# The first phase of a fused sparse-attention and ELU feed-forward kernel: eleven blocks' min-and-subtract step and one batch's v copies on GpSimd, with its DMA issues dealt out between them

## The chip, the cores and the metric

One core of a Trainium2 chip runs the whole program. The metric is device time in microseconds (us) of one execution; the time of a kernel is the median of its runs.

Five engines work side by side and meet only through semaphores: TensorE (PE, with its weight loads PEld), VectorE (DVE), ScalarE (ACT), GpSimd (POOL) and SyncE (SP). Each takes its own instructions strictly in order, so an instruction that waits holds up all that stand behind it on its engine. POOL and SP also issue DMAs; the transfers themselves run on 16 DMA engines.

## The reference

Attention over 8 batches, 8 heads, 576 positions, 64 features, followed by a feed-forward layer on its output. Heads 0 to 3 are local (a key is seen if it lies 0 to 31 positions back), heads 4 to 7 are strided (a key is seen if it lies a multiple of 32 positions back, or is the position itself).

```
scores = q @ k.T / 8, masked by head
attn   = softmax(scores);  x = attn @ v          # x: 4608 tokens x 512
h = x @ w_in                                      # 512 -> 2048
g = where(h > 0, h, exp(min(h, 0)) - 1)           # ELU
out = g @ w_out                                   # 2048 -> 512
```

## The kernel before

**Tiles and phases.** The 4608 tokens are nine chunks of 512. For a chunk `nb` the feed-forward layer has 16 blocks `m` of 128 hidden features. `moe_in` makes one block's hidden values `hps` in a PSUM bank with four 128x512 matmuls (L622); `moe_act` makes the ELU of it into `g_sb`; `moe_out` multiplies four blocks of `g_sb` at a time by `w_out_sb` (L667, four matmuls), and after four of those the result is copied (L671) and stored. A loop over `nb` and, inside, over slots `s` = 0 to 15 writes the order of all engines out by hand: in slot `s` comes block `m = s`, and two half-slots (`2s`, `2s+1`) of the next batch's attention, taken from the table `gaps` that `attention(nb + 1, ...)` makes. So while chunk 0 is worked on (the first phase), batch 1's attention runs between its blocks; batch 0's attention runs before the loop, in the hand-written order `OPENING`.

**The ELU of a block.** ACT makes `e_sb = exp(hps)` (L648). DVE then makes `e1_sb = min(e_sb, 1) - 1` (L655, the min and subtract step) and `g_sb = max(e1_sb, hps)` (L657). For five blocks of chunk 0, those in `ON_SCALAR` (4, 7, 10, 13, 15), it goes another way: ACT makes `e1_sb = relu(hps)` (L651) and DVE makes `min(e_sb - 1, e1_sb)` in one instruction (L652). `e_sb` and `e1_sb` have three buffers each.

**What ties PE to the others.** The banks for `hps` are a ring: three in slots 0 to 9 of chunk 0 (two "half" tiles and one "single"), two from slot 10 on. Block m's matmuls wait until the block that had the bank before has been through L657 or L652. In chunk 0 only the first three groups of `moe_out` are taken in the phase itself, at the ends of slots 11, 13 and 15 (they need blocks 0 to 3, 4 to 7 and 8 to 11); the fourth, which needs blocks 12 to 15, comes right after block 0 of chunk 1.

**The attention pieces.** A pair is two heads; `s0`, `s1` (strided) and `l0`, `l1` (local) for one batch. Pieces of a pair: transposes of q and k on PE (L361, L375) with copies out of PSUM (L364, L378), scores (L493) and their exp (L501, on ACT), the mask product on DVE (L516), the product with v (`av`, L535), its reciprocal and scaling on DVE (L543, L544, into `x_s` or `x_l`), and the transposes of that back on PE (L571, L584) with copies into `xT`. For the strided heads v is first copied from the landing tile `v_raw` into `v_str` (`v_in`, L414): for batch 1 on ACT, for later batches on DVE. `halo` (L421) copies the ends of local v rows.

**POOL's queue.** All loads but the first are issued from POOL in program order: strided tensors in five DMAs each (four of 108 rows, L178, and one for the rest, L182), local ones in one each (L189, L195), the weights `w_in_sb` in four slices (L316) and `w_out_sb` in four (L728). Eight semaphores go round among POOL's DMAs, so that each issue waits for the landing of the DMA eight places earlier. After batch 1's loads stand, in this order: the slices 2 and 3 of `w_in`, the four of `w_out`, memsets of batch 2's tiles (`clear_v(2)`, `clear_nat(2)`, L246 to L248 and L238), batch 2's loads (`load_batch(2)`, 18 DMAs), six small memsets (`clear_loc`, L243), batch 3's loads.

Of the kernel before, what the change touches and what calls it, by code (L numbers as in the profile page):

```python
# [13 lines left out]
ALU = mybir.AluOpType  # L14
# [28 lines left out]


OPENING = """
s0.cast_q s0.t_q s0.t_k s1.cast_q s1.t_k s0.s0 s0.m0 s1.t_q s0.s1 s0.m1 fill.2 l0.t_q s1.s1
s1.m1 s1.s0 s1.m0 l0.t_k l1.t_q fill.1 s0.v l0.s0 l0.m0 l1.t_k l0.s1 s1.a0 s0.a0 l0.m1 l1.s0
s1.a1 s0.a1 fill.1 l1.s1 l1.m0 fill.1 s1.halo s1.x fill.1 s0.x l1.m1 fill.1 l0.a0 fill.1 l0.a1
l1.a0 moe.2 l1.a1 S0.t_q l0.x S1.t_q moe.3 l1.x moe.0 moe.1
""".split()  # L50
ON_VECTOR = "s0.t_q s1.cast_q s1.t_k l0.t_q s0.v l1.x".split()


ON_SCALAR = (4, 7, 10, 13, 15)
AHEAD = 3


# [1 line left out]
def kernel(  # L59
# [9 lines left out]
    nc = tc.nc  # L69
    B, H, S, D = q.shape  # L70
# [93 lines left out]
    raw = {}  # L164
    src = {"q": q, "k": k, "v": v}

    def load_strided(b, name, engine=nc.gpsimd, heads=range(4)):
# [9 lines left out]
        for h in heads:  # L177
            engine.dma_start(out=t[0:108, h].rearrange("p g d -> p (g d)"),  # L178
                             in_=rows[h, :, 0:30, :].rearrange(
                                 "t (r g) d -> t r (g d)", g=5))  # L180
            if h == 1:
                engine.dma_start(  # L182
                    out=t[108:126, :, 0:2, :].rearrange("p h g d -> p h (g d)"),
                    in_=rows[:, :, 30:32, :].rearrange("h t g d -> t h (g d)"))

    def load_local(b, name):
        if name == "v":
# [35 lines left out]
    def load_batch(b):  # L223
        for name in "qkv":
            load_strided(b, name)
        for name in "qkv":
            load_local(b, name)

    def rows_of(t, h):

        return t[0:126, h, 0:2, :], t[0:108, h, 2:5, :]


    def clear_nat(i, engine=nc.vector):

        for name in "kq":
# [24 lines left out]
    for i in range(2):  # L261
# [17 lines left out]
                            op=ALU.subtract)  # L279
# [44 lines left out]
    load_local(1, "q")  # L324
    load_local(1, "k")
    load_local(1, "v")
    load_w_in(2)


    class Pair:  # L330
        def __init__(self, b, strided, hp):
            self.b, self.strided, self.hp = b, strided, hp
            self.kind = "s" if strided else "l"
            self.h2 = slice(2 * hp, 2 * hp + 2)
            self.name = f"{self.kind}{hp}"
            self.pr, self.x = {}, None

        def copy(self, step, late):

# [68 lines left out]

        def v_in(self, part):

            if self.strided and self.hp == 0:
                o = rows_of(v_str[self.b % 3][:, :, :, 0:D], slice(0, 4))[part]
                i = rows_of(raw[self.b], slice(0, 4))[part]
                self.copy("v", self.b > 1)(o, i)  # L414

        def halo(self):

# [172 lines left out]
    def attention(b, start, pitch, at):  # L590


        gaps = {}
        pairs = [Pair(b, s, hp) for s in (b < EARLY, b >= EARLY) for hp in range(2)]
        begin = start if b >= EARLY else [start + pitch * i for i in range(4)]
        if b >= EARLY:
            gaps[begin[0]] = [pairs[3].halo]
        for i, pr in enumerate(pairs):
            if b == 1 and pr.strided:
                pr.t_q = lambda: None  # L600
# [12 lines left out]


    g_of = {}
# [29 lines left out]
    def moe_act(nb, m):  # L645
        hps = hps_of[m]
        e_sb = p_e.tile([128, N_TILE], F32, tag="e_sb", name="e_sb")
        nc.scalar.activation(e_sb, hps, ACT.Exp)  # L648
        e1_sb = p_e.tile([128, N_TILE], BF16, tag="e1_sb", name="e1_sb")
        if nb == 0 and m in ON_SCALAR:  # L650
            nc.scalar.activation(e1_sb, hps, ACT.Relu)  # L651
            nc.vector.scalar_tensor_tensor(g_of[nb][:, m, :], e_sb, 1.0, e1_sb,  # L652
                                           op0=ALU.subtract, op1=ALU.min)
            return
        nc.vector.tensor_scalar(e1_sb, e_sb, scalar1=1.0, scalar2=1.0,  # L655
                                op0=ALU.min, op1=ALU.subtract)
        nc.vector.tensor_tensor(g_of[nb][:, m, :], e1_sb, hps, op=ALU.max)  # L657
# [49 lines left out]
    parts = [s for s in OPENING if s.startswith("moe")]  # L707
    for step in OPENING:
        pair, what = step.split(".")
        if pair == "fill":  # L710
            for _ in range(int(what)):
                nc.tensor.matmul(singles[3], lhsT=identity, rhs=mask_l[:, 0:512],
                                 start=True, stop=True)
            continue
        if pair == "moe":
            if step == parts[0]:

                ps_open.close()
                ps_h = inner.enter_context(tc.tile_pool(name="ps_h", bufs=1, space=PSUM))
                b_halves = [ps_h.tile([128, 512], F32, tag=f"half{i}", name=f"half{i}")  # L720
                            for i in range(2)]
                rings["hps"] = Ring(*b_halves, singles[3])
            moe_ahead(int(what), step == parts[0], step == parts[-1])
        else:
            pairs[pair].step(what)
    load_w_in(3)
    for i in range(4):
        nc.gpsimd.dma_start(out=w_out_sb[:, 4 * i:4 * (i + 1), :],  # L728
                            in_=wo[:, 4 * i:4 * (i + 1), :])
    clear_v(2, nc.gpsimd)  # L730
    clear_nat(2, nc.gpsimd)
    load_batch(2)
    for i in range(3):
        clear_loc(i, nc.gpsimd)
    opening.close()
    p_e = inner.enter_context(tc.tile_pool(name="elu", bufs=3))
    p_o = inner.enter_context(tc.tile_pool(name="o", bufs=3))
# [10 lines left out]
    for nb in range(n_chunks + 1):  # L748

        if nb + 1 < B:  # L750
            gaps = attention(nb + 1, *TIMES[min(nb + 1, 4)])
            if nb == 0:
                share([pair_a], b_halves + singles[3:], [], singles[:3])
            elif nb + 1 < EARLY:
                share([pair_a], b_halves, singles[3:], singles[:3])
            else:
                share([pair_a], b_halves + singles[:1], singles[3:], singles[1:3])
        else:
            gaps = {}
            share([], b_halves + singles[:1], singles[2:], singles[1:2])  # L760
        if nb + 3 < B:
            load_batch(nb + 3)
        for s in range(MC):
            if nb == 0 and s == 10:
                share([pair_a], b_halves, singles[3:], singles[:3])
            if s == 6 and nb > 0 and nb + 2 < B:
                transpose_batch(nb + 2)
            run(gaps, (2 * s,) if s else range(-10, 1))
            late = EARLY <= nb + 1 and s + 1 < MC
            if nb < n_chunks:  # L770
                moe_in(nb, s)
            if nb < n_chunks and not late:
                moe_act(nb, s)
            run(gaps, (2 * s + 1,) if s + 1 < MC else range(2 * s + 1, 1000))
            if nb < n_chunks and late:
                moe_act(nb, s)
            if nb == B and s == 4:
                range_flag(row_ok16)
            for chunk, i in outs(nb, s):
                moe_out(chunk, i)  # L780
        if nb + 1 == B:
            row_ok16 = range_check()

# [162 lines left out]
```

## Time and profile before

| | |
|---|---|
| median of 3 runs | 326.81 us (326.43 to 327.97) |
| profiled execution | 327.16 us, of which the profiled span is 325.3 us |
| PE busy | 301.5 us (93% of the span) |
| DVE busy | 243.3 us (75%) |
| ACT busy | 177.8 us (55%) |
| POOL busy | 131.4 us (40%), nearly all of it issuing DMAs |
| granted TensorE clock | 0.997 of full speed |

Rows of a timeline read: start in us from the span's start, length in us, engine, line, operation, output<-input, shapes, count; in square brackets, how long the engine had been idle before and what ended that. Rows with a count above 1 are neighbours put together, and their length is the whole of it. A matmul row ends later than the next may start, since matmuls are pipelined: four 128x512 matmuls show 1.03 us and let the next group start after 0.86 us. In an issue row the length is the time that POOL needs to issue the DMA, not the transfer.

### The profile page before, as it was taken

To read this page: it belongs to the slowest core of one execution; us is meant where nothing else is said; L and a number is where in the kernel's file an instruction comes from. 1 tells how busy PE (TensorE), PEld (TensorE's weight loads), DVE (VectorE), ACT (ScalarE), POOL (GpSimd) and SP (SyncE) were. 2 spreads that over 40 slices of the span, in tenths; PEclk is the share of its full clock that TensorE was granted. 3 is DMA by queue.
4 is the path that set the end of the run, shared out by engine and by line. 5 is a ranking of instruction groups with operands and counts; after the bars stand their busy time and mean duration, and the time that the engine had idled before them with its cause. 6 is when DMAs were issued, how large, how long until landed. Compare 5 with 4: busy or idle time off the path is not lost.

```text
span 325.3 us, 6088 instructions
## 1 busy us (share of the span) xinstructions
PE 301.5 (93%) x2205; PEld 150.8 (46%) x2246; DVE 243.3 (75%) x539; ACT 177.8 (55%) x337; POOL 131.4 (40%) x208
## 2 busy tenths in 40 slices
PE   2697888999999999999999999999999999999992
PEld 1463544555544554444444454454445444444440
DVE  6576887787888788988798879887887666866600
ACT  3577885776455664555555655555565444434320
POOL 9579825958389368839823830000000000000000
PEclk9999999999999999999999999999999999999998
DMA  6999999999999999999988992920210001100012
GB/s 112 154 169 120 168 207 139 148 130 162 158 141 97 106 154 172 139 182 169 148 117 143 148 135 62 153 83 35 55 48 32 33 34 54 43 35 33 32 67 72
DMA packets 102138, 35.67 MB, mean 110 GB/s; under 512 B 79885, under 2 KB 97493, under 8 KB 102101
## 3 DMA queue, kind: packets, MB, share of 16 engines
q0 software_dynamic: 67632, 18.10, 64.6%
q1 hardware_dynamic: 34469, 17.11, 24.8%
q8 instruction: 19, 0.31, 0.4%
q14 instruction: 18, 0.15, 0.2%
HBM read 36.70 MB, written 9.44 MB: 142 GB/s over the span
## 4 chain that ended last, share of the span: by engine, by line
PE 86%; DVE 4%; DMA 3%; ACT 3%; issue 2%; POOL 2%; ACTq 0%; POOLq 0%
PE single L667 38%; PE half L622 28%; PE single L622 9%; PE single L535 3%; DMA k_loc<-in_k_dram 3%; PE pair_a L456 2%; PE single L375 2%; PE single L571 1%; ACT e_sb L648 1%; PE pair_a L493 1%; DVE g_sb L657 1%; POOL k_str L178 1%; DVE x_l L544 1%; DVE x_s L544 1%; DVE g_sb L652 1%
## 5 line engine op out<-in xcount | busy, mean ns | idle before, releaser
L667 PE MATMUL single<-w_out_sb,g_sb 128*128 128x512 bf16 x558 | 143.6, 379 | 1.4 <-DVE g_sb L657 0.4
L622 PE MATMUL half<-xT,w_in_sb 128*128 128x512 bf16 x419 | 110.3, 379 | 1.1 <-issue 0.3
L648 ACT ACTIVATE e_sb<-half 128x512 f32<-128x512 f32 x109 | 65.3, 599 | 68.7 <-PE half L622 62.4
L655 DVE TENSOR_SCALAR e_sb<-e_sb 128x512 bf16<-128x512 f32 x139 | 62.0, 446 | 36.5 <-ACT e_sb L648 35.4
L667 PEld LDWEIGHTS <-g_sb 128*128 128x128 bf16 x576 | 53.5, 98 | 59.6 <-DVE g_sb L657 1.2
L622 PEld LDWEIGHTS <-w_in_sb 128*128 128x128 bf16 x576 | 51.7, 98 | 55.2 <-issue 0.2
L657 DVE TENSOR_TENSOR g_sb<-e_sb,half 128x512 bf16<-128x512 bf16 x104 | 71.5, 688 | 3.6
L622 PE MATMUL single<-xT,w_in_sb 128*128 128x512 bf16 x136 | 36.0, 379 | 0.3 <-issue 0.2
L648 ACT ACTIVATE e_sb<-single 128x512 f32<-128x512 f32 x35 | 21.1, 602 | 21.6 <-PE single L622 19.6
L671 ACT COPY o_sb<-single 128x512 f32<-128x512 f32 x36 | 21.1, 586 | 17.7 <-PE single L667 16.5
L535 PEld LDWEIGHTS <-pr 128*128 128x128 bf16 (+3 forms) x352 | 20.9, 105 | 15.0 <-issue 1.1
L178 POOL DMA_DIRECT2D v_raw<-in_v_dram x32 | 19.9, 659 | 15.8 <-DVE v_str L414 15.7
L462 ACT ACTIVATE pr<-pair_a 126x936 bf16<-126x936 f32 (+1 forms) x20 | 19.2, 962 | 11.8 <-PE single L456 11.8
L657 DVE TENSOR_TENSOR g_sb<-e_sb,single 128x512 bf16<-128x512 bf16 x35 | 24.1, 688 | 1.2
L178 POOL DMA_DIRECT2D k_str<-in_k_dram x32 | 20.1, 647 | 7.6 <-issue 3.6
L178 POOL DMA_DIRECT2D q_str<-in_q_dram x28 | 17.6, 651 | 6.3 <-DMA w_out_sb<-in_moe_w_out_dram 2.0
L544 DVE TENSOR_TENSOR x_l<-single,rden 96x384 bf16<-96x384 f32 x32 | 17.7, 554 | 1.1
L501 ACT ACTIVATE pr<-pair_a 128x576 bf16<-128x576 f32 (+2 forms) x20 | 13.1, 653 | 6.9 <-PE pair_a L493 6.9
L544 DVE TENSOR_TENSOR x_s<-single,rden 126x256 bf16<-126x256 f32 (+1 forms) x32 | 15.7, 491 | 1.1
L543 DVE RECIPROCAL rden<-single 96x6 f32<-96x6 f32 (+2 forms) x64 | 11.9, 185 | 3.6 <-PE single L535 3.2
L201 POOL DMA_DIRECT2D q_loc<-in_q_dram x16 | 12.3, 794 | 3.2 <-DMA k_str<-in_k_dram 1.6
L182 POOL DMA_DIRECT2D k_str<-in_k_dram x8 | 4.8, 606 | 19.4 <-PE single L375 6.3
(114 smaller groups left out, 269.0 us busy)
## 6 DMA issues: line engine op xcount, KB each, us to landing
out_dram<-o_sb SPq DMA_DIRECT2D x36, 256.0 KB, 2.2
v_loc<-in_v_dram POOLq DMA_DIRECT2D x8, 288.0 KB, 9.7
k_str<-in_k_dram POOLq DMA_DIRECT2D x32, 67.5 KB, 4.6
v_raw<-in_v_dram POOLq DMA_DIRECT2D x32, 67.5 KB, 4.4
w_in_sb<-in_moe_w_in_dram POOLq DMA_DIRECT2D x4, 512.0 KB, 9.2
w_out_sb<-in_moe_w_out_dram POOLq DMA_DIRECT2D x4, 512.0 KB, 16.7
q_str<-in_q_dram POOLq DMA_DIRECT2D x28, 67.5 KB, 6.9
q_loc<-in_q_dram POOLq DMA_DIRECT2D x4, 288.0 KB, 5.4
```

What stands on the lines that cost most here:

```text
L178: engine.dma_start(out=t[0:108, h].rearrange("p g d -> p (g d)"), in_=rows[h, :, 0:30, :].rearrange("t (r g) d -> t r (g d)", g=5))
L201: nc.gpsimd.dma_start(out=t[:, h // 2, 0:4, h % 2], in_=src[name][b, h, 0:512].rearrange("(i p) d -> p i d", p=128))
L462: nc.scalar.activation(both, sc[0:nk, :, 0:w], ACT.Exp, scale=scale)
L501: nc.scalar.activation(halves, sc[0:nk, :, 0:w], ACT.Exp, scale=scale)
L535: nc.tensor.matmul(av[0:m, p, blk - b0, :], lhsT=pr[0:nk, o:o + m], rhs=vt[0:nk, 2 * self.hp + p, blk, :], start=True, stop=True)
L544: nc.vector.tensor_tensor(self.x[0:nq, b0:b0 + n].rearrange("q g p d -> q p g d"), av[0:nq, :, 0:n, 0:D], r.unsqueeze(3).to_broadcast([nq, ...
L622: nc.tensor.matmul(hps, lhsT=w_in_sb[:, c, m * 128:(m + 1) * 128], rhs=xT[:, c, nb * N_TILE:(nb + 1) * N_TILE], start=start, stop=stop)
L648: nc.scalar.activation(e_sb, hps, ACT.Exp)
L655: nc.vector.tensor_scalar(e1_sb, e_sb, scalar1=1.0, scalar2=1.0, op0=ALU.min, op1=ALU.subtract)
L657: nc.vector.tensor_tensor(g_of[nb][:, m, :], e1_sb, hps, op=ALU.max)
L667: nc.tensor.matmul(ops, lhsT=g_of[nb][:, m, kk * 128:(kk + 1) * 128], rhs=w_out_sb[:, m, :], start=(m == 0), stop=(m == MC - 1))
L671: nc.scalar.copy(o_sb, ops)
```

## The change

Four things change, all in the first phase or ahead of it.

- For blocks 5 to 15 of chunk 0, L655 (or, in blocks 7, 10, 13 and 15, the relu on ACT and the joint instruction L652 on DVE) becomes a `tensor_scalar` min and subtract on POOL, followed by L657's max on DVE. Block 4 alone keeps the relu form.
- Batch 1's two `v_str` copies go from ACT to POOL, ahead of the last two `w_in` slices.
- POOL's issues are dealt out: `w_in` slices 2 and 3 and `w_out` slice 0 stand before the loop, `w_out` slices 1 to 3 in slots 5 to 7, and batch 2's loads from slot 9 on, one to three at a time; what is left of them, `clear_loc` and batch 3's loads follow at the phase's end.
- The memsets of batch 2's tiles go from POOL to DVE, into `OPENING`.

On POOL this gives the order: two copies, `w_in` 2 and 3, `w_out` 0, step 5, `w_out` 1, step 6, `w_out` 2, step 7, `w_out` 3, steps 8 and 9, one load, step 10, two loads, steps 11 and 12, two loads, step 13, three loads, step 14, one load, step 15, the rest ("step m" is the new instruction of block m; a load is one strided DMA of batch 2). The orders of PE and SP are the same as before.

```diff
-s1.m1 s1.s0 s1.m0 l0.t_k l1.t_q fill.1 s0.v ...
+s1.m1 s1.s0 s1.m0 clear.q clear.v l0.t_k l1.t_q fill.1 s0.v ...
...
-ON_SCALAR = (4, 7, 10, 13, 15)
+ON_SCALAR = (4,)
...
-    load_w_in(2)
...
         def v_in(self, part):
-            if self.strided and self.hp == 0:
+            if self.strided and self.hp == 0 and not (self.b == 1 and self.v_done):
                 o = rows_of(v_str[self.b % 3][:, :, :, 0:D], slice(0, 4))[part]
                 i = rows_of(raw[self.b], slice(0, 4))[part]
-                self.copy("v", self.b > 1)(o, i)
+                copy = nc.gpsimd.tensor_copy if self.b == 1 else self.copy("v", True)
+                copy(o, i)
...
+        if nb == 0 and m > 4:
+            nc.gpsimd.tensor_scalar(e1_sb, e_sb, scalar1=1.0, scalar2=1.0,
+                                    op0=ALU.min, op1=ALU.subtract)
+            nc.vector.tensor_tensor(g_of[nb][:, m, :], e1_sb, hps, op=ALU.max)
+            return
...
+        if pair == "clear":
+            clear_v(2) if what == "v" else clear_nat(2, names=what)
+            continue
...
-    load_w_in(3)
-    for i in range(4):
+    def load_w_out(i):
         nc.gpsimd.dma_start(out=w_out_sb[:, 4 * i:4 * (i + 1), :],
                             in_=wo[:, 4 * i:4 * (i + 1), :])
-    clear_v(2, nc.gpsimd)
-    clear_nat(2, nc.gpsimd)
-    load_batch(2)
-    for i in range(3):
-        clear_loc(i, nc.gpsimd)
+    pairs["S0"].step("v")
+    load_w_in(2)
+    load_w_in(3)
+    load_w_out(0)
+    third = batch_steps(2)
...
             for chunk, i in outs(nb, s):
                 moe_out(chunk, i)
+            if nb == 0 and 5 <= s < 8:
+                load_w_out(s - 4)
+            if nb == 0 and s > 8:
+                for _ in range(1 + (s > 11)):
+                    next(third)
+        if nb == 0:
+            for _ in third:
+                pass
+            for i in range(3):
+                clear_loc(i, nc.gpsimd)
+            load_batch(3)
```

`batch_steps` is `load_batch` as a generator that stops after each DMA, and once more after the second head of a tensor; so of the five stops of a tensor one issues two DMAs and one issues none. `clear.k`, not shown, stands behind `s0.m0`.

More of the change, by code (lines that the diff above doesn't have):

```diff
@@ L45 @@
 OPENING = """
-s0.cast_q s0.t_q s0.t_k s1.cast_q s1.t_k s0.s0 s0.m0 s1.t_q s0.s1 s0.m1 fill.2 l0.t_q s1.s1
-s1.m1 s1.s0 s1.m0 l0.t_k l1.t_q fill.1 s0.v l0.s0 l0.m0 l1.t_k l0.s1 s1.a0 s0.a0 l0.m1 l1.s0
+s0.cast_q s0.t_q s0.t_k s1.cast_q s1.t_k s0.s0 s0.m0 clear.k s1.t_q s0.s1 s0.m1 fill.2 l0.t_q s1.s1
+s1.m1 s1.s0 s1.m0 clear.q clear.v l0.t_k l1.t_q fill.1 s0.v l0.s0 l0.m0 l1.t_k l0.s1 s1.a0 s0.a0 l0.m1 l1.s0
 s1.a1 s0.a1 fill.1 l1.s1 l1.m0 fill.1 s1.halo s1.x fill.1 s0.x l1.m1 fill.1 l0.a0 fill.1 l0.a1
@@ L165, with strided_steps @@
     src = {"q": q, "k": k, "v": v}
-    def load_strided(b, name, engine=nc.gpsimd, heads=range(4)):
+    def strided_steps(b, name, engine=nc.gpsimd):
         rows = src[name][b, 4:8].rearrange("h (t r) d -> h t r d", r=STRIDE)
@@ L176, in load_strided @@
             t = nat[name, "str"][b % 3].rearrange("p (h g d) -> p h g d", h=4, d=D)
-        for h in heads:
+        for h in range(4):
             engine.dma_start(out=t[0:108, h].rearrange("p g d -> p (g d)"),
@@ L184, in load_strided @@
                     in_=rows[:, :, 30:32, :].rearrange("h t g d -> t h (g d)"))
+                yield
+            yield
+    def load_strided(*args):
+        for _ in strided_steps(*args):
+            pass
     def load_local(b, name):
@@ L221, in transpose_batch, with batch_steps, load_batch, clear_nat @@
                         in_=nat[name, "loc"][b % 3][:, 640 * a:640 * a + 640])
-    def load_batch(b):
+    def batch_steps(b):
         for name in "qkv":
-            load_strided(b, name)
+            yield from strided_steps(b, name)
         for name in "qkv":
             load_local(b, name)
+            yield
+    def load_batch(b):
+        for _ in batch_steps(b):
+            pass
     def rows_of(t, h):
         return t[0:126, h, 0:2, :], t[0:108, h, 2:5, :]
-    def clear_nat(i, engine=nc.vector):
-        for name in "kq":
+    def clear_nat(i, engine=nc.vector, names="kq"):
+        for name in names:
             t = nat[name, "str"][i].rearrange("p (h x) -> p h x", h=4)
@@ L336, in __init__ @@
             self.pr, self.x = {}, None
+            self.v_done = False
         def copy(self, step, late):
@@ L599, in attention @@
             if b == 1 and pr.strided:
-                pr.t_q = lambda: None
+                pr.t_q, pr.v_done = lambda: None, True
             for off, piece in ((at[0], pr.t_q), (at[1], pr.t_k),
@@ L760 @@
             share([], b_halves + singles[:1], singles[2:], singles[1:2])
-        if nb + 3 < B:
+        if 0 < nb and nb + 3 < B:
             load_batch(nb + 3)
@@ L780 @@
                 moe_out(chunk, i)
+            if nb == 0 and 5 <= s < 8:
[5 more added lines that the diff above has]
+            for _ in third:
+                pass
+            for i in range(3):
+                clear_loc(i, nc.gpsimd)
+            load_batch(3)
         if nb + 1 == B:
```

## The prediction

> **What bounds the kernel now.** I read the page first: which engine is full, and where it isn't.
>
> ```profile
> span 325.3 us, 6088 instructions
> PE   2697888999999999999999999999999999999992
> ...
> ACT  3577885776455664555555655555565444434320
> ```
>
> One slice is 8.1 us. From the eighth slice on (57 us) PE is at 9 tenths or more to the end, and nothing of the change lies there but what it makes late. So at stake is the time until about 57 us, in which PE still has gaps. The chain of waits says who makes them: between 29 and 55 us it hops between ACT's exps and copies, DVE's L655 and L657, and PE; batch 1's v copies stand on it with 1.36 us. The timeline of PE in the first phase then gives the gaps one by one. These are the ones behind block 8:
>
> ```profile
> 40.64 1.04 PE L622 MATMUL single<-xT,w_in_sb 128*128 128x512 bf16 x4
> 41.88 0.30 PE L493 MATMUL pair_a<-qT_loc,kT_loc 64*128 64x96 bf16 x6 [0.21 <-ACT pr L501]
> ...
> 43.10 0.32 PE L571 MATMUL single<-identity,x_s 108*128 108x108 bf16 x3 [0.69 <-DVE x_s L544]
> ...
> 48.02 0.30 PE L493 MATMUL pair_a<-qT_loc,kT_loc 64*128 64x96 bf16 x6 [0.31 <-ACT pr L501]
> ...
> 54.34 0.30 PE L584 MATMUL single<-identity,x_l 96*128 96x96 bf16 x3 [0.80 <-DVE x_l L544]
> ...
> 57.34 1.03 PE L667 MATMUL single<-w_out_sb,g_sb 128*128 128x512 bf16 x4
> ```
>
> With one of 0.16 at 45.50 they make 0.21 + 0.69 + 0.16 + 0.31 + 0.80 = 2.2 us. The last row is the fourth `moe_out`, my end mark: it needs block 15's `g_sb`, and behind it PE has no gaps left. Why I count from block 8 on only is seen in the weight loads and in POOL's queue:
>
> ```profile
> 40.63 0.55 PEld L622 LDWEIGHTS <-w_in_sb 128*128 128x128 bf16 x4 [0.17 <-DMA w_in_sb<-in_moe_w_in_dram]
> ```
> ```profile
> 40.88 0.87 POOL L182 DMA_DIRECT2D q_str<-in_q_dram  x1 [0.92 <-DMA w_in_sb<-in_moe_w_in_dram]
> 43.37 0.57 POOL L178 DMA_DIRECT2D q_str<-in_q_dram  x1 [1.62 <-DMA w_in_sb<-in_moe_w_in_dram]
> 45.91 0.57 POOL L178 DMA_DIRECT2D q_str<-in_q_dram  x1 [1.97 <-DMA w_out_sb<-in_moe_w_out_dram]
> ```
>
> Block 8 is the first to use `w_in` slice 2, and it started as that slice landed. The issues behind it wait for the next slices, about 2.5 us apart, so the transfers go one after the other without a break.
>
> **Ahead of block 8: nothing gained.** ACT loses two v copies (1.36 us) and block 7's relu (0.6), DVE three L655 (0.43 each, one of them 0.96). PE would come to block 8 a little earlier and wait there. Slice 2 lands no earlier, since the same bytes stand before it. Nor later: its issue comes behind two POOL copies. Bounds for those: POOL's 32x256 memsets start 0.26 us apart, 1.0 ns an element, so 512 + 768 elements take 1.3 us; by the 128x128 affine select (0.29 us, 2.3 ns an element) 2.9 us. The issue moves from 30.4 to 32 or 33.5 us; the slice ahead of it in the queue, v of the local heads, landed at 38.9 (the POOL issue waiting for it went at 39.17). The cover is over 5 us; beyond it each microsecond would cost one. The memsets put on DVE in the opening (0.59 for k behind `s0.m0`; 0.59 and about 0.4 behind `s1.m0`) fall into DVE's idle times of 0.91 and 1.51 us there. Cost 0.
>
> **From block 8 on: POOL's queue.** DVE loses L655 for blocks 8, 9, 11, 12 and 14 (5 x 0.43 = 2.1 us), ACT the relus of 10, 13 and 15 (3 x 0.6 = 1.8 us). In their place stands a step on POOL, and DVE's L657 waits for it with reciprocals, scalings and masks queued behind it; PE waits for those at the gaps above. And POOL's steps stand in one queue with its issues, whose price the trace has:
>
> ```profile
> 54.37 1.17 POOL L178 DMA_DIRECT2D k_str<-in_k_dram  x2 [0.16 <-issue]
> ```
>
> So 0.6 us an issue. In the order of the change POOL has, from block 12's exp on: step 12, two issues, step 13, three issues, step 14, one issue, step 15. With P for a step that is 4P + 6 x 0.6 = 4P + 3.6 us in a row. Block 12's exp ran from 50.51 to 51.11. Then L657 of block 15 (0.69) and three handovers of 0.05 each (L655 of block 12 started 0.03 behind its exp) are to be added, and the fourth `moe_out` starts at 51.11 + 0.05 + 4P + 3.6 + 0.05 + 0.69 + 0.05 = 55.55 + 4P, against 57.34 now. Even is P = 0.45.
>
> **The price of P.** No POOL row is a `tensor_scalar`. The rows nearest:
>
> ```profile
> 1.02 0.29 POOL masks.py:199 TENSOR_SCALAR_AFFINE_SELECT identity<-identity 128x128 bf16<-128x128 bf16 x1
> ...
> 61.50 0.31 POOL L243 MEMSET k_loc<- 32x256 bf16 x1
> 61.76 0.31 POOL L243 MEMSET q_loc<- 32x256 bf16 x1
> ```
>
> A memset only writes: 0.26 us for 256 elements, 0.5 for 512. The affine select reads, computes and writes, and makes its pattern beside: 0.29 for 128, so 4 x 0.29 = 1.16 for 512 at most, and 0.9 if 0.09 of it is a fixed part. I take 0.8, nearer to the row that reads too. Then 55.55 + 3.2 = 58.75: **1.4 us late**. Slots 9 to 11 just keep pace with that: exp 9 ends at 45.46, three steps and three issues are 4.2 us, L657 of block 11 is through at 50.4, and block 13, which takes its bank, started at 50.45.
>
> One more term: L421, the halo copy on DVE (41.13 us), now runs beside steps on POOL. DVE's L655 shows what that can do:
>
> ```profile
> 37.19 0.96 DVE L655 TENSOR_SCALAR e_sb<-e_sb 128x512 bf16<-128x512 f32 x1
> ...
> 39.40 0.43 DVE L655 TENSOR_SCALAR e_sb<-e_sb 128x512 bf16<-128x512 f32 x1
> ```
>
> The first ran beside a POOL memset (36.71 to 37.87) and took 0.53 us longer. Behind L421 stand the scalings that PE waits for at 43.10. Bounds 0 and 0.5, taken 0.2. The Trainium skill, "SBUF — State Buffer", on the intuition of a bandwidth pool, has it that GpSimd and a two-port DVE instruction can't run together, one blocks the other; the pair of rows agrees, and by that rule the halo copy could wait for a whole step, 0.8 instead of 0.2. Sum: 1.4 + 0.2 = **1.6 us slower**.
>
> **Behind the phase: nothing.** Step 15 ends at 51.16 + 3.2 + 3.6 = 57.96; then come one k and five v loads of batch 2, the last at 57.96 + 5 x 0.6 = 60.96 (now 57.8). Such a load took 2.3 to 3.9 us to land: 63.3 to 64.9. DVE's copy of it, now at 61.95, would be due near 63.5: up to 1.4 us of waiting. Behind it stands L657 of block 2 of chunk 1 (63.29 to 63.98), whose bank PE needs at 65.05: a cover of 1.1 us, so at worst 0.3 comes through; I take 0. Local q and k (landed 64 and 67, used at 70.6 and 72.1) and batch 3's transposes (the second issued by 80.0, median 8.3 us to landing, used at 93.95) have 3 us or more.
>
> **The rivals.**
>
> *POOL is as quick as its memsets: no change.* P = 0.5 gives 55.55 + 2.0 = 57.55, 0.2 late, and block 12's exp comes up to 0.5 earlier, since steps 9 to 11 are shorter: 0 in all, 326.8 us. For it: POOL's memset of 32x1280 (1.16 us) is even 0.9 ns an element. Against: a memset reads nothing. The Trainium skill, "GPSIMD Engine Reference", section on engine selection, says that one-input elementwise work on GpSimd runs at about line rate; as an estimate from its 1.2 GHz, 512 elements take 0.43 us, and by that the sum is 57.27, no change. Chance 0.20.
>
> *Faster: POOL's issues don't hold its steps up.* If a step can start while a DMA is still being issued, the 3.6 us fall away, DVE and ACT are lighter by 2.1 and 1.8 us, and PE's gaps of 2.2 us can close: 324.6 us. Deciding point: POOL's stretch behind exp 12 below 5.4 us. For it: the relief of DVE and ACT is as large as the gaps, and all of `w_out` lands in time for it (the issue that waits for the fourth slice went at 53.62). Against: POOL's rows follow each other without overlap, issue behind issue 0.6 apart, and memset behind issue. Chance 0.12.
>
> *Much slower: a step at 1.0 us or more.* At P = 1.16 slots 9 to 11 need 5.3 us, block 13 is 1.0 late, and the end mark goes to 55.55 + 1.0 + 4.64 = 61.2: 3.9 us late, 330.7 us. Chance 0.20.
>
> **How the numbers follow.** The likeliest case (0.48) is P between 0.6 and 1.0: 0.6 to 2.2 us late without the halo, 1.6 with my values. The profiled execution goes from 327.16 to 328.8; it was 0.35 over the median of the runs, so 326.81 becomes 328.4. The range takes in no change and most of both outer rivals: from 1.4 faster (325.4) to 4.0 slower (330.8). 0.5%, about what a measurement can tell here, is 1.6 us. Faster by more: the second rival, 0.12. Within: the first rival (0.20) and P below 0.8 of the likeliest (0.22), 0.42. Slower by more: 0.26 and 0.20, 0.46.
>
> **What would show it.** Right: block 8 again at 40.6; POOL without idle time from step 12 to step 15, and L657 of blocks 13 to 15 waiting for it; the fourth `moe_out` near 58.8; no gaps behind. The price of a step is read from POOL's rows at once. Wrong: a step of 0.45 us or less, block 8 far from 40.6, or a wait in chunk 1 that I put at nothing.

## The result: 4.6% slower, and the profile after

The changed kernel takes 342.47 us (median of 6 runs, 338.81 to 343.66) against 326.63 us before (6 runs on the same chip): a ratio of 1.046, 95% interval 1.041 to 1.050. That is 15.8 us slower, where 1.6 were forecast and 4.0 were the worst in the range. The profiled execution took 340.33 us with a span of 338.4, that is 13.1 more span than before; the accounts below are made in it.

From the page of the changed kernel (its line numbers: L663 is the new step on POOL, L665 the max behind it on DVE, L684 `moe_out`, L634 `moe_in`; L672 and L674 are the old step and max, still used for blocks 0 to 3 and from chunk 1 on):

```profile
span 338.4 us, 6090 instructions
...
PE   1887767788999999999999999999999999999993
...
PEclk9999958999999999999999999999999999999999
...
PE 76%; POOL 7%; DMA 6%; DVE 6%; issue 2%; ACT 2%; ACTq 0%; POOLq 0%; DVEq 0%
...
L663 POOL TENSOR_SCALAR e_sb<-e_sb 128x512 bf16<-128x512 f32 x11 | 21.3, 1936 | 6.4 <-ACT e_sb L660 3.3
...
L665 DVE TENSOR_TENSOR g_sb<-e_sb,half 128x512 bf16<-128x512 bf16 x9 | 6.2, 686 | 15.8 <-POOL e_sb L663 15.8
```

The price of a step is in the fifth row: **1.94 us**, where I took 0.8 and put 1.16 as the upper bound. The sixth says who pays: DVE sat idle 15.8 us in front of nine of its maxes, all for POOL. PE reaches 9 tenths in the eleventh slice (85 us) for good, instead of the eighth (57 us), and in the sixth and seventh its granted clock is below full.

POOL's timeline from block 11's step to block 15's shows the queue that the prediction drew: after step 12 no idle time at all, only longer.

```profile
54.56 1.94 POOL L663 TENSOR_SCALAR e_sb<-e_sb 128x512 bf16<-128x512 f32 x1
56.72 1.92 POOL L663 TENSOR_SCALAR e_sb<-e_sb 128x512 bf16<-128x512 f32 x1 [0.22 <-ACT e_sb L660]
58.58 1.27 POOL L178 DMA_DIRECT2D q_str<-in_q_dram  x2
59.85 1.96 POOL L663 TENSOR_SCALAR e_sb<-e_sb 128x512 bf16<-128x512 f32 x1
61.74 1.28 POOL L178 DMA_DIRECT2D k_str<-in_k_dram  x2
62.96 0.64 POOL L182 DMA_DIRECT2D k_str<-in_k_dram  x1
63.59 1.98 POOL L663 TENSOR_SCALAR e_sb<-e_sb 128x512 bf16<-128x512 f32 x1
65.47 0.68 POOL L178 DMA_DIRECT2D k_str<-in_k_dram  x1
66.17 1.95 POOL L663 TENSOR_SCALAR e_sb<-e_sb 128x512 bf16<-128x512 f32 x1
```

PE's timeline gives the new gaps (the number in brackets is how long PE stood still):

```profile
44.91 0.45 PE L583 MATMUL single<-identity,x_s 108*128 108x108 bf16 x3 [2.60 <-DVE x_s L556]
...
54.77 0.30 PE L596 MATMUL single<-identity,x_l 96*128 96x96 bf16 x3 [1.15 <-DVE x_l L556]
57.27 1.77 PE L634 MATMUL half<-xT,w_in_sb 128*128 128x512 bf16 x4 [1.14 <-DVE g_sb L665]
...
63.28 0.30 PE L596 MATMUL single<-identity,x_l 96*128 96x96 bf16 x3 [1.26 <-DVE x_l L556]
66.34 1.02 PE L634 MATMUL half<-xT,w_in_sb 128*128 128x512 bf16 x4 [1.03 <-DVE g_sb L665]
68.90 0.39 PE L684 MATMUL single<-w_out_sb,g_sb 128*128 128x512 bf16 x1 [0.61 <-DVE g_sb L665]
76.62 0.33 PE L547 MATMUL single<-v_str,pr 126*128 126x65 bf16 x4 [0.91 <-DVE pr L528]
77.68 1.02 PE L634 MATMUL half<-xT,w_in_sb 128*128 128x512 bf16 x4 [0.45 <-DVE g_sb L674]
```

The first row is the gap of 0.69 us that the prediction shows at 43.10, grown to 2.60; the last two lie behind the stretch in which it counted gaps. The releasers named are DVE's, but DVE itself waited: with 1.08, 1.95, 0.98 and 0.96 us for the steps of blocks 5 to 8, with 1.80, 2.37 and 1.87 for those of 13 to 15, and then with 3.63 for a load:

```profile
75.94 0.29 DVE L426 COPY v_str<-v_raw 126x512 bf16<-126x512 bf16 x1 [3.63 <-DMA v_raw<-in_v_dram]
```

To read where the time is lost I compare, block by block, when PE begins a block's weight loads. Later than in the profile of before, in us: block 8 of chunk 0 -0.8; block 9 +2.2; block 12 +5.5; block 15 +9.0; block 1 of chunk 1 +10.9; block 8 of chunk 1 +12.6; from chunk 3 on +13.3. So 2.2 are lost ahead of block 9, 8.7 by the end of the phase, 1.7 in chunk 1, and 0.7 later.

### The profile page after: what moved, and what is told of

Read it like the earlier page. It is cut to its first block, busy times and chain, and to the rows that moved or that the text cites. A ratio compares the mean times of both kernels' runs of the same rounds, so it can differ in the third digit from the quotient of the medians.

```text
span 338.4 us, 6090 instructions
## 1 busy us (share of the span) xinstructions
PE 306.7 (91%) x2205; PEld 152.4 (45%) x2246; DVE 242.1 (72%) x537; ACT 175.3 (52%) x331; POOL 150.8 (45%) x216
## 4 chain that ended last, share of the span: by engine, by line
PE 76%; POOL 7%; DMA 6%; DVE 6%; issue 2%; ACT 2%; ACTq 0%; POOLq 0%; DVEq 0%
PE single L684 34%; PE half L634 25%; PE single L634 8%; POOL e_sb L663 4%; PE single L547 3%; DMA q_str<-in_q_dram 2%; DMA v_raw<-in_v_dram 2%; PE pair_a L468 2%; DVE g_sb L674 2%; DMA k_str<-in_k_dram 1%; PE single L386 1%; POOL k_str L178 1%; DVE e_sb L672 1%; PE single L583 1%; ACT e_sb L660 1%
## 5 line engine op out<-in xcount | busy, mean ns | idle before, releaser
L684 PE MATMUL single<-w_out_sb,g_sb 128*128 128x512 bf16 x558 | 144.4, 380 | 2.2 <-DVE g_sb L665 0.6
L634 PE MATMUL half<-xT,w_in_sb 128*128 128x512 bf16 x419 | 112.6, 386 | 4.1 <-DVE g_sb L665 2.4
L672 DVE TENSOR_SCALAR e_sb<-e_sb 128x512 bf16<-128x512 f32 x132 | 58.9, 446 | 33.8 <-ACT e_sb L660 33.0
L684 PEld LDWEIGHTS <-g_sb 128*128 128x128 bf16 x576 | 53.7, 98 | 60.8 <-DVE g_sb L665 1.1
L634 PEld LDWEIGHTS <-w_in_sb 128*128 128x128 bf16 x576 | 52.3, 99 | 60.2 <-issue 6.4
L674 DVE TENSOR_TENSOR g_sb<-e_sb,half 128x512 bf16<-128x512 bf16 x99 | 68.1, 688 | 3.5
L634 PE MATMUL single<-xT,w_in_sb 128*128 128x512 bf16 x136 | 35.9, 379 | 0.3 <-issue 0.2
L663 POOL TENSOR_SCALAR e_sb<-e_sb 128x512 bf16<-128x512 f32 x11 | 21.3, 1936 | 6.4 <-ACT e_sb L660 3.3
L674 DVE TENSOR_TENSOR g_sb<-e_sb,single 128x512 bf16<-128x512 bf16 x33 | 22.7, 688 | 1.1
L178 POOL DMA_DIRECT2D k_str<-in_k_dram x32 | 20.2, 647 | 6.8 <-DMA k_loc<-in_k_dram 2.5
L665 DVE TENSOR_TENSOR g_sb<-e_sb,half 128x512 bf16<-128x512 bf16 x9 | 6.2, 686 | 15.8 <-POOL e_sb L663 15.8
```

Of the source, the lines that this page charges most:

```text
L634: nc.tensor.matmul(hps, lhsT=w_in_sb[:, c, m * 128:(m + 1) * 128], rhs=xT[:, c, nb * N_TILE:(nb + 1) * N_TILE], start=start, stop=stop)
L663: nc.gpsimd.tensor_scalar(e1_sb, e_sb, scalar1=1.0, scalar2=1.0, op0=ALU.min, op1=ALU.subtract)
L684: nc.tensor.matmul(ops, lhsT=g_of[nb][:, m, kk * 128:(kk + 1) * 128], rhs=w_out_sb[:, m, :], start=(m == 0), stop=(m == MC - 1))
```

## Experiments

The theory: the step's price on POOL, 1.94 us, made the loss, through the queue of steps and issues and through DVE's waiting for it. Rivals: the dealing out of the issues costs by itself; the loads, copies and memsets that moved do; the price is not the step's own but comes of sharing the memory with DVE; the lowered TensorE clock makes the time; and, near the end, the handover over a third engine costs whatever its price.

This table is for reading them: how much later than in the profile of before a block's weight loads begin (us; c1 is chunk 1), and the ratio of times with its interval.

| run | block 8 | block 9 | block 15 | c1, block 1 | c1, block 8 | median us | ratio |
|---|---|---|---|---|---|---|---|
| the change | -0.8 | 2.2 | 9.0 | 10.9 | 12.6 | 342.47 | 1.041 to 1.050 |
| e1_step_back | -0.5 | -1.0 | -1.0 | -1.0 | -1.0 | 326.86 | 0.996 to 1.003 |
| e2_quarter_step | -0.4 | 0.4 | 3.4 | 3.4 | 4.7 | 332.32 | 1.011 to 1.026 |
| e2_half_step | 0.3 | 1.7 | 5.8 | 6.2 | 8.1 | 334.29 | 1.014 to 1.028 |
| e5_fill_gaps | 0.7 | 2.8 | 9.2 | 10.5 | 12.3 | 340.00 | 1.032 to 1.044 |
| e6_from_block_9 | 0.5 | 0.6 | 6.5 | 8.4 | 11.1 | 336.03 | 1.021 to 1.032 |
| e7_not_dealt | 24.7 | 26.2 | 31.7 | 33.6 | 33.6 | 360.97 | one run |
| v2_copies_and_half_slices | -0.1 | 1.3 | 2.3 | 2.3 | 2.3 | 328.90 | 1.002 to 1.008 |
| e8_copy_for_step | -0.3 | -0.3 | 0.2 | 0.2 | 1.9 | 329.31 | 1.006 to 1.014 |
| e9_v_loads_sooner | -0.1 | -0.3 | 2.2 | 3.8 | 3.8 | 329.31 | 1.003 to 1.010 |
| v3_half_slices | -0.5 | -0.4 | -0.4 | -0.4 | -0.4 | 327.07 | 0.999 to 1.002 |

How far profiles of one and the same program differ is seen in e3_prices, which up to its last chunk is the kernel before: 0.4 to 0.7 in these five columns. A difference below 1 us in the table says little by itself.

The kernel before, run beside them, took 327.08 to 327.35 in these sessions.

### The step taken back

```diff
-ON_SCALAR = (4,)
+ON_SCALAR = (4, 7, 10, 13, 15)
...
-        if nb == 0 and m > 4:
-            nc.gpsimd.tensor_scalar(e1_sb, e_sb, ...)
-            nc.vector.tensor_tensor(g_of[nb][:, m, :], e1_sb, hps, op=ALU.max)
-            return
```

> The changed kernel with the eleven steps back on DVE and the relus of blocks 7, 10, 13 and 15 back on ACT, as before; the v copies on GpSimd, the dealt-out issues and the moved memsets stay. Theory A (the price of a step on POOL, 1.94 us by the profile of the changed kernel, fills POOL's queue and all else follows from it): within 0.5% of before, 325.0 to 328.3 us, and batch 2's loads land as early as before. Rival B (the dealing out itself, with batch 2's loads between the slots and its remainder after the phase, costs the time): most of the 16 us stays, 335 us or more. Rival C (the lower granted clock in the first phase comes from the loads or the v copies): the clock stays under 1 between 40 and 60 us.

Measured: 326.86 us, no difference from before. So everything else in the change (issues dealt out, v copies on POOL, memsets on DVE) together costs nothing that can be measured, and the whole loss hangs on the step. The granted clock was 1.00 from 40 to 60 us, so the loads and copies don't lower it either. In its profile PE was 1.0 us early from block 9 into chunk 2, and had lost that again by chunk 3.

### Part of the step on POOL

```diff
-            nc.gpsimd.tensor_scalar(e1_sb, e_sb, ...)
+            for eng, cols in ((nc.gpsimd, slice(0, 128)), (nc.vector, slice(128, 512))):
+                eng.tensor_scalar(e1_sb[:, cols], e_sb[:, cols], ...)
```

> The changed kernel, with each step on POOL for 128 of the 512 columns only and on DVE for the other 384; the order of all else is that of the change. Theory A: if a step's price goes by its columns it falls to about 0.5 us, and the sum of the prediction, 55.55 + 4P for the fourth group of the output matmuls, gives 57.6, as before within a microsecond: 326 to 328.5 us. Rival B: the issues stand between the steps as in the changed kernel, so the loss stays over 10 us.

> As the quarter step, with 256 of the 512 columns on POOL: a step of about 1.0 us. Theory A by the prediction's sum: slots 9 to 11 0.5 us late, then 55.55 + 0.5 + 4 = 60.1 for the fourth group of the output matmuls, 2.7 us late: 329.4 us, 328 to 332. Rival B: over 10 us late, as much as with the whole step.

Measured: 332.32 and 334.29 us; POOL's part took 0.82 and 1.21 us. The direction is as expected, but the times lie 3.8 and 2.3 us above the ranges. The run doesn't vary the price alone: DVE keeps a part of every step, so that its relief is mostly gone while it still waits for POOL, and the gap ahead of block 9 comes back with the price (0.4 and 1.7 us). My expectation had nothing for that gap, nor for the loss in chunk 1 and the clock (0.71 and 0.66 of full speed granted from 45 to 50 us). For the quarter step that isn't all: by the table it loses 3.0 us between blocks 9 and 15, where the sum over POOL's queue has less than 1, and why isn't shown. The clean test of the price is e8, below.

### The price by itself

Twelve POOL instructions behind the last block of chunk 8 of the kernel before, with no work left on DVE beside them:

```diff
+            two = dict(scalar1=1.0, scalar2=1.0, op0=ALU.min, op1=ALU.subtract)
...
+            p.memset(f_a, 0.5)
+            p.tensor_copy(h_b, f_a)
+            p.tensor_scalar(h_b, f_a, scalar1=1.0, scalar2=None, op0=ALU.min)
...
+            p.tensor_scalar(h_b, f_a, **two)
...
```

> The kernel before, with a row of POOL instructions added at the very end of the last chunk, each on 128 partitions, for their prices alone; the output is not touched. Theory A: min and subtract from f32 to bf16 on 512 columns near 1.9 us without any DVE work beside it; 256 and 128 columns in proportion (1.0, 0.5); a copy of 512 near 0.6, by the v copies of the changed kernel (1.48 us for 512 and 768 elements together). If the price goes by the number of operations, one operation takes about half of two, 1.0 us. Rival D (the step is slow because DVE works beside it): 0.5 to 1.0 us for the full step here.

The groups of POOL, busy time, then mean ns of one. L793 is the step as the change has it, L791 the min alone, L796 and L797 the step on 256 and 128 columns, L799 a two-input subtract, L790 a plain copy from f32, L789 a memset:

```profile
L793 POOL TENSOR_SCALAR h_b<-f_a 128x512 bf16<-128x512 f32 x1 | 1.9, 1928 | 0.1
...
L791 POOL TENSOR_SCALAR h_b<-f_a 128x512 bf16<-128x512 f32 x1 | 1.5, 1516 | 0.1
...
L799 POOL TENSOR_TENSOR h_b<-h_a,f_a 128x512 bf16<-128x512 bf16 x1 | 1.2, 1159 | 0.1
L796 POOL TENSOR_SCALAR h_b<-f_a 128x256 bf16<-128x256 f32 x1 | 1.1, 1064 | 0.1
L797 POOL TENSOR_SCALAR h_b<-f_a 128x128 bf16<-128x128 f32 x1 | 0.6, 637 | 0.1
L790 POOL CAST h_b<-f_a 128x512 bf16<-128x512 f32 x1 | 0.6, 612 | 0.1
...
L789 POOL MEMSET f_a<- 128x512 f32 x1 | 0.5, 523 | 0.0
```

With DVE at rest the step takes 1.93 us, the same as in the middle of the phase: sharing with DVE isn't what makes it dear. (Parts of a step did take longer beside DVE's own part: 0.63 to 1.29 us for 128 columns and 1.08 to 1.45 for 256 in the two runs above, against 0.64 and 1.06 here.) It costs 3.4 ns a column beyond some 0.2 us, (1928 - 637) / 384; a copy of the same tile is three times as quick, and dropping one of the two operations saves only 0.4. The affine select of the prediction (0.29 for 128 columns) is less than half of this instruction's 0.64 for 128: it was no upper bound.

### The clock kept up

Idle matmuls put on PE into the new gaps (before the transposes that wait, and before blocks 13, 14, 15 and the first of chunk 1), nothing else changed:

```diff
+                    nc.tensor.matmul(bank[:, 320:512], lhsT=identity, rhs=mask_l[:, 0:192], ...)
...
+            if (nb, s) in ((0, 13), (0, 14), (0, 15), (1, 0)):
+                for _ in range(4):
+                    nc.tensor.matmul(pair_a[:, 0, :], lhsT=identity, rhs=mask_l[:, 0:512], ...)
```

> The changed kernel with idle matmuls (their results are not used) put on PE where it waits in the first phase: 24 of 192 columns before the second part of the x_s transposes of batch 1's second strided pair, 10 before the second part of each local pair's, 4 of 512 columns before blocks 13, 14, 15 and block 0 of chunk 1. Theory C (PE's granted clock, 0.57 to 0.79 between 42 and 60 us in the changed kernel, is itself a part of the loss: the groups of blocks 9, 10 and 12 or 13 took 1.8 us instead of 1.04, and block 9's exp waits for them): the clock stays near 1 and the time falls by about 2 us, to 340.5. Theory A alone (POOL's queue sets the pace, slow matmuls are hidden behind it): no change within 1 us, 341.5 to 343.5.

Busy times by window, with the granted clock behind POOL's; first the changed kernel:

```profile
45.00:52.00 7.00, 6.47 (x56) 3.60 (x57) 2.61 (x6) 3.66 (x7) 4.29 (x4) 0.60 0.95 155
...
57.00:60.00 3.00, 2.55 (x11) 1.19 (x12) 1.94 (x5) 0.60 (x1) 2.99 (x4) 0.57 0.02 1
```

and with the filling matmuls:

```profile
45.00:52.00 7.00, 4.75 (x60) 2.72 (x59) 3.60 (x9) 3.56 (x7) 5.73 (x5) 1.00 1.09 179
...
57.00:60.00 3.00, 3.00 (x19) 1.47 (x19) 1.55 (x4) 0.60 (x1) 3.00 (x4) 1.00 0.10 4
```

The clock is back at 1.00 in every window from 42 to 80 us, and the fourth `moe_out` starts at 67.55 instead of 67.42: by the span the end of the phase comes no sooner. But block 8 began 1.5 us later here than in the changed kernel; counted from it, block 1 of chunk 1 comes 1.9 us sooner. The median is 340.0, 2.5 lower; the intervals of the two ratios overlap, so whether the clock is worth those 2.5 us or nothing isn't settled.

### Only from block 9 on

```diff
-ON_SCALAR = (4,)
+ON_SCALAR = (4, 7)
...
-        if nb == 0 and m > 4:
+        if nb == 0 and m > 8:
```

> The changed kernel with the step on POOL for blocks 9 to 15 only; 5 to 8 on DVE, 7 with its relu, as before. Theory A with the measured price of 1.94: block 9 starts about 3 us behind the landing of the third w_in slice, as before, and the fourth group of the output matmuls at 66 to 67 (slots 9 to 11 3.4 us late, then 55.55 + 3.4 + 7.76 = 66.7): 337 to 340 us, so blocks 5 to 8 cost some 2 to 4 us of the 16, which the prediction had at nothing. Rival (what lies ahead of block 8 is free, as the prediction had it): as the changed kernel, 342.5.

Measured: 336.03 us, 1 us below the expected range. Without the steps of blocks 5 to 8 the 2.2 us at block 9 shrink to 0.6, and the fourth `moe_out` starts at 65.20 instead of 67.42. By the medians these four steps cost 6.4 us, by the two profiled executions 2.0 (338.38 against 340.33; here it is the slowest of five). That they cost something is shown, how much only as 2 to 6. The other seven cost most of the rest. DVE's copy of v waited 4.6 us here.

### The issues not dealt out

```diff
-    load_w_out(0)
-    third = batch_steps(2)
+    for i in range(4):
+        load_w_out(i)
+    load_batch(2)
...
-                load_w_out(s - 4)
...
-                    next(third)
...
```

> The changed kernel, all eleven steps on POOL, but the last three w_out slices and batch 2's 18 loads issued in one row ahead of the steps, as before the change. Theory A (POOL's queue): step 5 waits for the last of these issues, which went at 59.8 us in the kernel before, so it starts near 61 us instead of 35.7; then eleven steps of 1.94 with nothing between take 21 us, to 82 at least, and the fourth group of the output matmuls follows near 83 instead of 67.4: 355 to 360 us. Rival B (dealing out is what costs): faster than the changed kernel.

Measured: 360.97 us in one run. The first step on POOL started at 61.14 us instead of 35.71, behind all the issues and the transfers that they wait for. Given a step on POOL, the dealing out is worth some 18 us by this one run (360.97 less 342.47), in which the granted clock was 0.68 to 0.69 from 30 to 90 us; the dealing out is not what costs.

### The copies and a sliced load, without the step

The kernel before with the v copies of batch 1 on POOL and `w_in` slice 2 in two DMAs of 256 columns; the memsets of batch 2's tiles stay on POOL.

```diff
-    load_w_in(2)
+    for w in (slice(1024, 1280), slice(1280, 1536)):
+        nc.gpsimd.dma_start(out=w_in_sb[:, :, w], in_=wi[:, :, w])
...
-                self.copy("v", self.b > 1)(o, i)
+                copy = nc.gpsimd.tensor_copy if self.b == 1 else self.copy("v", self.b > 1)
+                copy(o, i)
...
```

> The kernel before, with batch 1's two v copies on POOL behind the third w_in slice, and that slice in two DMAs of 256 columns. No ELU step on POOL. Theory A: the copies cost POOL 1.5 us where it has room, ACT loses 1.36 us that stands on the chain ahead of block 8, and block 8, which starts as its weights land, gets them up to 1.25 us earlier: block 8 0.5 to 1.3 us earlier relative to the landing of the first w_out slice, 0.5 to 1.5 us faster: 325 to 326.5. Rival: the gain ahead of block 8 is lost at the next landing or to noise: 326.5 to 327.5.

Measured: 328.90 us, 0.5% slower, and above both of the expected ranges. Its timeline shows why: the two POOL memsets of 1.16 us now lie at 38.13 and 39.24, and DVE's `tensor_scalar` that began at 39.43 beside the second took 1.25 us instead of 0.43. The scaling behind it came late, PE waited 1.52 us for it at 43.96, and block 9 was 1.3 us later. Block 10 was already 2.3 later: the granted clock was 0.78 from 45 to 50 us, and block 9's four matmuls took 1.89 us instead of 1.04.

### The price alone changed

```diff
-            nc.gpsimd.tensor_scalar(e1_sb, e_sb, scalar1=1.0, scalar2=1.0,
-                                    op0=ALU.min, op1=ALU.subtract)
+            nc.gpsimd.tensor_copy(e1_sb, e_sb)
```

> The changed kernel with a plain copy (f32 to bf16, 128x512) on POOL where it has the min and subtract step; min and subtract of blocks 5 to 15 of chunk 0 are left out. Queue order, issues, waits and the work on DVE and ACT stay as they are; only the step's price changes, to 0.61 us by the probe of the cast at the end of the kernel before. If the sum over POOL's queue is right and the price alone was wrong: the end mark at 55.55 + 4 x 0.61 = 58.0 us, 0.7 behind the kernel before, PE's granted clock near 1.00 from 40 to 80 us, nothing lost in chunk 1, and a time of 326.5 to 328.5. If the handover over POOL and the waits of DVE for another engine cost by themselves, whatever the step's price: 332 or more, with DVE waits on POOL in front of PE's gaps as before. If the relief of ACT and DVE counts for something and the price alone hid it: under 326.

Measured: 329.31 us, 13.2 less than the change. The step took 0.61 and the fourth `moe_out` started at 57.53, 0.2 later than before. Block 15's max ended at 57.83, where the prediction's formula, without its last 0.05, has 55.50 + 4 x 0.61 = 57.94. Part of that agreement is luck: step 12 began 0.4 us sooner than the formula has it, and POOL stood idle for 0.47 ahead of step 15, for block 15's exp. So with a step of this price the phase is on time, and the handover costs nothing more at its end. The granted clock was 1.00 in every window from 40 to 80 us, so the 13.2 us also hold what the lowered clock costs, which comes with the gaps. But the time is 0.8 us above the range that I gave, and the profile says where that comes from: chunk 1. First DVE, then PE:

```profile
65.03 0.40 DVE L426 COPY v_str<-v_raw 126x512 bf16<-126x512 bf16 x1 [3.40 <-DMA v_raw<-in_v_dram]
```
```profile
65.81 0.33 PE L547 MATMUL single<-v_str,pr 126*128 126x65 bf16 x4 [0.78 <-DVE pr L528]
66.97 1.02 PE L634 MATMUL half<-xT,w_in_sb 128*128 128x512 bf16 x4 [0.56 <-DVE g_sb L673]
```

The last load of v is issued at 59.89, 2.1 us later than before, since steps stand in front of it, and takes 5.0 us to land instead of 3.4; why it takes longer isn't shown. DVE waits for it in order, with the maxes of chunk 1 behind.

### The v loads sooner

```diff
-                for _ in range(1 + (s > 11)):
+                for _ in range(2):
                     next(third)
```

> The run with the plain copy on POOL in place of the step (min and subtract of blocks 5 to 15 of chunk 0 left out), and in it two of batch 2's issues a slot from slot 9 on, where there was one in slots 9 to 11: the v loads come three issues, some 1.8 us, sooner. In the run with the plain copy alone the end mark was 0.2 us later than before, yet block 8 of chunk 1 was 1.9 later: DVE waited 3.4 us for the last load of v (landed 65.0 us), with L673 of the blocks of chunk 1 queued behind it, and PE waited 0.78 and 0.56. If that wait is what it lost: DVE's copy of v starts by 63.5 us, PE has no such gaps, block 8 of chunk 1 comes near 75.3, and the time is 326.8 to 328.2. If the loss lies elsewhere (the waits of DVE on POOL in the first phase, or work shifted in chunk 1 whatever the loads do): 329 to 330, as without the change.

Measured: 329.31 us, no better. The wait in chunk 1 is gone: DVE's copy (at 65.14) waits for no load, and block 8 of chunk 1 is no later than block 1. But this doesn't prove the theory. The profile (330.94 us, 1.6 above the median) is 3.8 us late by then, so the copy comes due that much later, and the last load wasn't issued sooner at all: at 60.46, against 59.89 in e8. What is lost is lost in the phase. From POOL and from PE:

```profile
53.77 0.59 POOL L182 DMA_DIRECT2D k_str<-in_k_dram  x1 [1.01 <-DVE x_l L556]
```
```profile
56.45 0.42 PE L596 MATMUL single<-identity,x_l 96*128 96x96 bf16 x3 [2.29 <-DVE x_l L556]
```

The releaser named in the first row isn't the right one. By its operands this issue waits for the semaphore of the DMA eight issues before it, `w_out` slice 3, which landed at 53.48. So an issue brought forward meets the transfer that still runs on its semaphore, block 13's step stands behind it on POOL, and DVE's next scaling behind that. Behind the gap the granted clock was 0.52 from 57 to 60 us, and two groups of four matmuls took 1.91 and 1.79 us instead of 1.03. In neither of the two orders tried were the loads early and the steps in time.

### The half slices alone

e1's kernel with `w_in` slice 2 in two DMAs, as in the diff of v2.

> The changed kernel with its POOL step taken back (relu on ACT for blocks 4, 7, 10, 13 and 15, the rest on DVE, as before the change), and w_in slice 2 loaded in two DMAs of 256 columns. Without the split block 8 started at 40.11 us, as the slice landed at 40.07, while PE was ready for it about 1 us sooner by the block before. With the split blocks 8 and 9 need only the first half, which lands about 1.3 us sooner; one more issue of 0.6 us on POOL stands ahead of q, k and v of batch 2. If the landing of slice 2 holds the phase: 0.5 to 1 us faster than before, 325.5 to 326.5, if chunk 1 does not lose it again as it did without the split. If blocks 5 to 7 are held by DVE and ACT just as long: no difference, 326.5 to 327.5.

Measured: 327.07 against 327.08 us. The first half landed 0.7 us sooner than the whole slice in e1 (39.37 against 40.07), and block 8 began at 40.16 regardless, as blocks 5 to 7 came 0.6 to 1.0 us later than in e1. PE waited for nothing just ahead of block 8; why the blocks before it came later isn't shown, and in e3_prices block 5 came 2.0 us sooner than in the same program's other profile. No version here beats the kernel before.

## Why the prediction was wrong

**"The price of P"** is the step that failed: 0.8 us taken, 0.5 and 1.16 as bounds, 1.94 measured; with 0.61 in its place (e8) 13.2 of the 15.8 us were gone. The bounds were a memset and a select of a quarter of the columns, and neither is this instruction; I treated the dearest row at hand as an upper end, though nothing in the trace tied it to a `tensor_scalar`.

**"From block 8 on: POOL's queue"** held in its structure, but its end mark was misread. Not all of the fourth `moe_out` needs block 15: only the last of its four matmuls reads that block's `g_sb`. Before, the first one began at 57.34, when block 15 wasn't through yet:

```profile
56.66 0.69 DVE L652 SCALAR_TENSOR_TENSOR g_sb<-e_sb 128x512 bf16<-128x512 f32 x1 [1.33 <-ACT e_sb L651]
```

The last one began at 57.99 before, and at 68.90 in the changed kernel, where it stands as a row by itself above. So the sum had to be held against 57.99: with P = 0.8 it says 0.8 us late and not 1.4, and even is P = 0.61. With 1.94 in it, slots 9 to 11 need 3 x 1.94 + 1.8 = 7.6 us instead of the 4.2 that just kept pace, 3.4 late, and the sum goes to 55.55 + 3.4 + 7.76 = 66.7, 8.7 late. With the 2.2 us that block 9 was late already that is 68.9, as measured, and 10.9 late in all, as in the table. No idle time from step 12 to 15, and L665 of blocks 13 to 15 waiting, came as said.

**"Ahead of block 8: nothing gained"** was right for block 8 itself (39.85, not 40.6) but wrong in its cost of 0. I counted the relief of DVE and ACT there, and no later term had the new wait: DVE stood still for the steps of blocks 5 to 8, and the scaling of the strided heads behind L665 came at 44.29 instead of 42.48. PE waited 2.60 us for it. With a step of 0.61 this gap is 0.99 and block 9 is on time; so this term, too, follows the price. Two readings in that part were off, and nothing rests on them: DVE loses two L655 there (blocks 5 and 6), not three; and slice 2 did land earlier, at 38.60 instead of 40.59 (40.07 in e1, with the same queue ahead of it).

**The halo term** (0.2 us) was not there: the halo copy ran from 41.99 inside the step from 41.50 to 43.43 and took 0.49 us as before. The rule that the prediction cited, from the Trainium skill, "SBUF — State Buffer" (intuition of a bandwidth pool), that GpSimd and a two-port DVE instruction can't run together, isn't borne out by this pair, if the halo copy is such an instruction, which no run here shows. One mask product that began with a step (54.63) did take 0.87 us instead of 0.45, while the others inside a step took 0.42 to 0.50; and beside POOL's memset (DVE's `tensor_scalar` in v2, 1.25 us for 0.43) the trace agrees with the rule.

**"Behind the phase: nothing"** was wrong by 1.7 us in chunk 1, and this doesn't hang on the price alone: e8 has it with a step of 0.61. I gave the last v load 2.3 to 3.9 us to land and DVE's copy a wait of up to 1.4; in e8 it took 5.0 (issued at 59.89, the copy started at 65.03), and the wait was 3.4. This is read from the profiles; no run takes that wait away and leaves the rest in time. Of the cover of 1.1 us nothing was left. Some 0.7 us more are lost at chunk 3, where PE waits 0.49 for a scaling at 147.52 us; why there isn't shown.

**The rivals.** "Much slower" had the right mechanism with the wrong end: its own formula, on the prediction's mark, gives 3.9 us at 1.16 and 9.4 at 1.94. "As quick as its memsets" falls with the first row of the price: the rule that it leaned on beside (the Trainium skill, "GPSIMD Engine Reference", section on engine selection, one input at about line rate, 0.43 us by my estimate) is 0.18 short for the plain copy's 0.61 and off by 4.5 times for this `tensor_scalar`. "POOL's issues don't hold its steps up" falls with POOL's timeline: step and issue follow each other without overlap of more than 0.1.

What isn't settled: the median is 15.8 us above before, the profiled execution 13.2. The six executions of the changed kernel had granted clocks of 0.967 to 0.985, the quickest of them the highest, but the slowest not the lowest; the clock may be part of it.

## What to carry to other kernels

Price an operation on GpSimd by a row of that very instruction; a memset, a select or a copy of the same tile says nothing on it, and where no such row exists the upper bound is open and the range must say so. When a step moves to an engine that also issues the DMAs, follow three things: the engine that waits for the step with its queue behind it (from the first such step on, not from the point where the bound seems to begin), the DMAs that now stand behind the steps, and the work that waits for their landing a phase later. In these runs the handover was free at the phase's end with a step of 0.61 us, and not with one of 1.94.

## What the runs showed of the hardware

- A `tensor_scalar` on GpSimd, 128x512, took 1.93 us with two operations and 1.50 with one, the same for f32 and bf16 in and out (1.92 to 1.93), and the whole step took the same alone as beside DVE; a copy took 0.61, a memset 0.52, a two-input subtract 1.16. That a two-input operation is quicker than one with a scalar I had not expected.
- Gaps of 1 to 3 us in PE's work cost its clock as well: 0.57 to 0.79 of full speed granted in the windows around the widest of them, four matmuls in 1.89 us instead of 1.04, and 1.00 again with idle matmuls in the gaps. The Trainium skill, "TensorE: Matmul & The Clock Gate", Part 1, tells of a gate that halves the clock after an idle window of about 3.4 us; the trace agrees in kind after a stretch (42 to 45 us) in which PE was busy for 0.38 of 3 us, but the 0.57 from 57 to 60 us came behind two standstills of only 1.15 and 1.14 us, for which that window doesn't account. The experiments have it too, behind gaps of 1.52 (v2) and 2.29 us (e9), so part of what a gap costs comes after it.
- An issue that was brought forward (e9) waited 1.01 us for the transfer eight issues ahead of it, and the profile named another releaser for that.
